# Windowed attention and a gated MLP on one core: the scores of packs 1 to 4 from 128-row products, and another order of the first exponent passes

## Chip, cores and metric

One Trainium2 chip, one core of it. The number is the device time of one execution in microseconds (us); each kernel is run several times and the median stands for it. A profiled execution gives the trace that the rows below come from.

## What is computed

The reference, cut to what matters. The inputs are q, k, v of shape (8, 8, 576, 64) and three weights of 512 x 1536 and 1536 x 512, all float32.

```python
window, dilation, scale = 32, 4, 1.0 / np.sqrt(64)
scores = scale * np.matmul(q, k.transpose(0, 1, 3, 2))
rel = pos[:, None] - pos[None, :]
mask_plain = (rel >= 0) & (rel < window)
mask_dil = (rel >= 0) & (rel < window * dilation) & (rel % dilation == 0)
# heads 0 to 3 use mask_plain, heads 4 to 7 mask_dil
attn = softmax(np.where(masks, scores, -1e9))
x = (attn @ v).transpose(0, 2, 1, 3).reshape(4608, 512)
g = x @ w_gate
out = (g * sigmoid(g) * (x @ w_val)) @ w_out
```

## The kernel before, in words

**Attention comes in packs.** A pack is a tile of queries and keys of four heads: two halves (partitions 0 to 63 and 64 to 127 hold the 64 features of one half each), four blocks of 32 queries in each half, each against its 64 keys. Packs alternate between the plain and the dilated heads. The code counts them from 0 (`m`), and so does this text. For one pack, `scores` adds a mask to the bank `two` by two products with an identity (for the first six packs) and then makes 32 small products of 64 rows, 32 queries and 63 keys. `shift` takes the row maximum away, `exps` exponentiates, `turn_e` transposes on TensorE, `keys` copies the transposed tile out of PSUM, `results` makes 32 products with the values, `norm` divides, `turn_y` transposes on VectorE, and `x_copy` writes the high and the low part of x. A float32 product of this kind is two weight loads and two matmuls in the trace.

**The MLP comes in items.** An item is 512 columns of x (256 in the first six) times 128 columns of the gate and value weights (`gv_mm` into banks `bg`, `bv`) and then times the output weights (`out_mm` into the four banks `bo`). Each product is done in three terms of high and low parts. Weights arrive as bit patterns in units `u` of 128 x 1536 words. Five stages turn a unit into high and low parts: E (exponent, ScalarE), T and B (shift and bits), H (high part, ScalarE), L (low part, GpSimd or VectorE). Item t needs units 2t and 2t+1 for t below 3.

**What sets the order.** Up to the first item's products the order is written by hand: the string `START` is read from left to right, one letter a step (q, v and w issue loads on SyncE's queue, Q scores, S shift, X exps, T turn_e, K keys, A results, N norm, U turn_y, H and L the parts of x, W the next stage of a weight unit, I and J products on a dummy bank). After that, the class `Desk` takes all the instructions in the order of the code and reorders those of every engine but TensorE by its own costs and due times; TensorE keeps the order of the code. In that code `attend(now)` stands between the products of the items: `EARLY`, `LATER` and the lists behind them say at which `now` a pack's visits A (results of the pack before, scores of this one), B (transposes) and C (copies) stand. `Desk.used` remembers for every 32 bytes of a tile's columns who wrote them last, without regard to partitions, and makes a later writer wait for that one.

**Loads.** A load on SyncE's queue waits for the one eight before it on the same queue (eight semaphores in turn), and for whatever still reads its target. The tile of queries and keys of packs 0, 2, 4, 5 is one place, that of packs 1 and 3 another.

Of the kernel before, what the change touches and what calls it, by code (L numbers as in the profile page):

```python
# [12 lines left out]
I32 = mybir.dt.int32  # L13
# [5 lines left out]
P = 128  # L19
# [38 lines left out]

NCS = 3
NSTART = 2  # L60
HALVED = 3
WARM = 9
TURNED = 20
FREE = 16000, 19500, 17500, 18000, 6000
EARLY = (-1, 1, None), (2, 4, 3), (5, 8, 6)
MASKED = 6
X_LOW, W_LOW, H_LOW, KEYS = (3, 7), (1, 5), (5,), (2,)
ON_ACT = (2, 3, 4, 5, 6, 9, 11, 12, 15, 17, 19, 21, 23)
START = ("q0 q1 w v0 v1 w Q0 Q1 S0 X0 T0 W0 I3 I2 S1 K0 X1 W1 A0 W2 T1 J2 K1 W3 J2 N0 W0 w U0 q2 v2 A1 q3 w w r W4 H0 "
         "L0 N1 U1 H1 L1 W1 v3 W2 W3 W4")  # L70
LATER = (14, 3, 2), (23, 3, 4), (29, 7, 4), (39, 3, 2)
T0 = NPLAIN * CH
# [9 lines left out]
class Pack:  # L82
# [5 lines left out]
    def __init__(self, half, strided, part, rest=0):  # L88
        self.half, self.strided, self.part, self.rest = half, strided, part, rest
        self.tail = half == NB  # L90
        self.step = DIL if strided else 1
        self.qstep = BQ
        n = BQ
        if not strided:
            if self.tail:
                self.at = [[(4 * part + 2 * i + g // 2, CH + BQ * (g % 2), 96 * (g // 2) + BQ * (g % 2)) for g in range(NG)]
                           for i in range(2)]
            else:
                self.at = [[(half, 256 * part + P * i + BQ * g, BQ * g) for g in range(NG)] for i in range(2)]
        elif self.tail:  # L100
            n, self.qstep = BQ // 2, BQ // 2
            self.at = [[(4 * rest + g, CH + 2 * part + i, 48 * g) for g in range(NG)] for i in range(2)]
        elif half == 0:
            self.at = [[(0, 2 * i + g // 2 + 256 * part + P * (g % 2), 96 * (g // 2) + BQ * (g % 2)) for g in range(NG)]
                       for i in range(2)]
        else:
            self.at = [[(half, 2 * part + i + DIL * BQ * g, BQ * g) for g in range(NG)] for i in range(2)]
        self.n = n
        self.qwidth = self.qstep * (NG - 1) + BQ
        self.kwidth = max(k for _, _, k in self.at[0]) + BK  # L110
        self.cols = NH * (self.qwidth + self.kwidth)
        first = ["".join("oF"[q < BQ * self.step] for _, q, _ in x) for x in self.at]
        self.mask = MASKS.index(first[0])
        self.mask_step = 0 if first[1] == first[0] else NG
        assert MASKS[self.mask + self.mask_step:][:NG] == first[1]

    def q_at(self, g, j):
        return self.qwidth * j + self.qstep * g

    def k_at(self, i, g, j):  # L120
        return NH * self.qwidth + self.kwidth * j + self.at[i][g][2]
# [13 lines left out]


PACKS = packs()
NPK = len(PACKS)
QKB = max(x.cols for x in PACKS)

# [13 lines left out]
class Desk:  # L154
# [28 lines left out]
    def places(self, ap):  # L183

        t, size = ap.tensor, mybir.dt.size(ap.dtype)
        key = t.name, ap.offset, tuple(map(tuple, ap.ap)), size
        if key not in self.found:
            blocks = ()
            if not isinstance(t, bass.DRamTensorHandle):
                blocks = 0,  # L190
                if ap.space == bass.MemoryType.DRAM:
                    blocks = ap.offset // (P * PIECE),
                elif ap.space != bass.MemoryType.PSUM:
                    at = np.zeros(1, np.int64) + ap.offset % ap.ap[0][0]
                    for step, n in ap.ap[1:]:
                        at = (at[:, None] + step * np.arange(n)).reshape(-1)
                    blocks = tuple(np.unique(at * size // 32).tolist())
                if t.name not in self.users:
                    self.users[t.name] = {}
                    r = getattr(t, "manual_sbuf_range", None) or (0, 0)  # L200
                    self.span[t.name] = r
                    self.under[t.name] = [x for x, (a, e) in self.span.items() if a < r[1] and r[0] < e and x != t.name]
                    for x in self.under[t.name]:
                        self.under[x].append(t.name)
            self.found[key] = t.name, blocks
        return self.found[key]
# [120 lines left out]
def attention_moe(ctx, tc, qkb, vb, w, const, out):  # L327
# [80 lines left out]
    raw_of = {}  # L408
    YW = 3 * UT + 8

    def w_load(parts=2):
        nonlocal loaded
        u = loaded
        n = u % 5 if u < NU - NLAST else (u - NU + NLAST) % NRAW
        if u >= NU or raw_of.get(n, -1) >= done["B" if u < NU - 1 else "L"]:
            return False
        raw_of[n] = u
        loaded += 1
        t = at(raw_at[n], 2 * WU, I32)
        n = 2 * WU // parts  # L420
        for k in range(parts):
# [125 lines left out]
    def masks_of(m, i):  # L547
        n = BK * (pk(m).mask + i * pk(m).mask_step)
        return mask_sb[:, n:n + BK * NG].rearrange("q (g k) -> q g k", g=NG)[:, :, 1:]

    def scores(m, two, masked):

        t = st[m]["qk"]
# [17 lines left out]
    def shift(m, two, pool, masked):  # L571
        mx = pool["bm"](2 * NG).rearrange("q (i g) -> q i g", i=2)
        e = pool["e"]()
        ev = e.rearrange("q (g i k) -> q i g k", g=NG, i=2)[:, :, :, 1:]
        s = two[:, :, SA:].rearrange("q i (g k) -> q i g k", g=NG)
        if not masked:
            n = BK * pk(m).mask
# [225 lines left out]
    nc.vector.memset(ones, 1.0)  # L803
    nc.vector.memset(some, 0.0)
    nc.scalar.activation(out=some, in_=some, func=AF.Exp)
    clear_e(early)
    nc.vector.tensor_copy(out=ident16, in_=eye)
    for n, x in enumerate(MASKS[:4]):
        nc.vector.tensor_copy(out=mask_sb[:, BK * n:BK * n + BK], in_=two_masks[:, BK * "Fo".index(x):][:, :BK])
# [4 lines left out]
    def idle(n, bank=k_bank[1]):  # L814
# [19 lines left out]
        "w": lambda m: w_load(3), "r": lambda m: ready.update(w=True), "I": lambda n: idle(n), "J": lambda n: idle(n, k_bank[0]), "W": lambda n: w_one(STAGES[n]),  # L834
    }

    et = mybir.EngineType
# [39 lines left out]
    def attend(now):  # L877
        for what, m in visit.get(now, ()):
            r = ended(m)
            if what == "A":  # L880
                if r is not None:
                    results(r, two)
                if m < NPK:
                    scores(m, two, m < MASKED)
                if r is not None:
                    norm(r, two, pool_of(r))
# [13 lines left out]
            elif what == "B":  # L900
                if TURNED <= m < NPK:
                    turn_far(m, later)
                elif m < NPK:
                    turn_e(m, two[:, 1])
                    keys(m, two[:, 1], pool_of(m))
            elif r is not None:
                x_copies(r)

# [226 lines left out]
    for t, it in enumerate(items):  # L1135
# [8 lines left out]
        mixing(t, 0)  # L1144
        if not late and t:
            out_mm(before, False)
        gv_mm(it, 1)
        dve_h(it)
        h_hi(it)
# [56 lines left out]
def layout(q, k, v, moe_w_gate, moe_w_val, moe_w_out):  # L1206
# [3 lines left out]
    for m, pk in enumerate(PACKS):  # L1210
        for i, blocks in enumerate(pk.at):
            for g, (b, q0, _) in enumerate(blocks):
                qt = q0 + pk.step * np.arange(pk.n)
                kt = q0 + pk.step * np.arange(-BQ, BQ)
                a, e = int((kt < 0).sum()), int((kt < S).sum())
                for j in range(NH):
                    h, r, qc, kc = NH * pk.strided + j, D * i, pk.q_at(g, j), pk.k_at(i, g, j)
                    qkb[m, r:r + D, qc:qc + pk.n] = q[b, h, qt].T
                    qkb[m, r:r + D, kc + a:kc + e] = k[b, h, kt[a:e]].T
                    vb[m, r + a:r + e, NH * g + j, :D] = v[b, h, kt[a:e]]  # L1220
# [28 lines left out]
```

## Time and profile before

| | |
|---|---|
| median of 3 runs | 911.08 us (909.94 to 911.4) |
| profiled execution | 914.47 us, its span 912.7 us |
| TensorE (PE) busy in the span | 897.8 us, 98% |
| VectorE (DVE), ScalarE (ACT), GpSimd (POOL) busy | 646.0, 382.5, 257.8 us |
| granted TensorE clock, mean | 0.996 of full |

The busy time of TensorE is 98% of the span, so what counts is the time in which it waits or runs at the lower clock; the other engines matter where TensorE waits for them. 1.8 us of the profiled time lie around the span.

### The profile page before, as it was taken

The page shows a single profiled execution, that of the slowest core. Times are in us where ns is not written, and L with a number is a line of the kernel's source. Part 1 is how long each engine was busy: PE and PEld are TensorE (multiplying, and loading weights), DVE is VectorE, ACT ScalarE, POOL GpSimd, SP SyncE. Part 2 cuts the span into 40 slices and gives each one's busy share as a digit, 9 for nine tenths or more (in the row PEclk, how much of TensorE's full clock was granted, in tenths as well). Part 3 has the DMA queues.
Part 4 walks back from the last instruction along what each step waited for, and adds up shares of the span by engine and source line. Part 5 has one row for each costly group of instructions (what it writes and reads, how often), then busy time and mean ns, then how long its engine had stood idle before and what let it go on. Part 6 is the DMA issues. An engine that isn't in the chain of part 4 may idle for free.

```text
span 912.7 us, 20897 instructions
## 1 busy us (share of the span) xinstructions
PE 897.8 (98%) x8642; PEld 737.0 (81%) x8642; DVE 646.0 (71%) x993; ACT 382.5 (42%) x593; POOL 257.8 (28%) x177
## 2 busy tenths in 40 slices
PE   6899999999999999999999999999999999999998
PEld 4798888888888888888888888888878888888886
DVE  5687779888795473777789766878787746555752
ACT  4788433333243242333336544333345533334452
POOL 2468712221311112012032630111146501213451
PEclk9899999999999999999999999999999999999999
DMA  9899986453464640887888678989866675565562
GB/s 338 326 337 368 373 287 224 153 184 122 164 239 146 211 162 13 265 288 263 291 272 282 233 247 279 306 279 296 273 211 222 212 240 198 188 199 189 193 223 92
DMA packets 90382, 214.24 MB, mean 235 GB/s; under 512 B 9264, under 2 KB 32432, under 8 KB 90288
## 3 DMA queue, kind: packets, MB, share of 16 engines
q1 hardware_dynamic: 79776, 208.09, 66.2%
q10 hardware_dynamic: 10512, 4.82, 2.0%
q8 instruction: 68, 1.11, 0.5%
q14 instruction: 26, 0.21, 0.1%
HBM read 165.69 MB, written 47.19 MB: 233 GB/s over the span
## 4 chain that ended last, share of the span: by engine, by line
PE 96%; DMA 2%; issue 1%; SPq 0%; ACT 0%; DVE 0%; POOL 0%; ACTq 0%
PE bo L250 43%; PE bg L250 23%; PE bv L250 23%; PE two L250 7%; DMA at_int<-w 1%; DMA at_float<-turned 1%; SPq L234 0%; DVE at_float L250 0%; POOL at_float32r L234 0%; ACT at_float32r L250 0%; ACT at_float32r L234 0%; ACT at_float L250 0%; ACT at_int L234 0%; ACTq L234 0%
## 5 line engine op out<-in xcount | busy, mean ns | idle before, releaser
L250 PE MATMUL bo<-at_float32r 128*128 128x512 f32 x1296 | 305.7, 390 | 0.0
L250 PEld LDWEIGHTS bo<-at_float32r 128*128 128x128 f32 x1296 | 242.6, 188 | 51.0
L250 POOL TENSOR_TENSOR at_float32r<-at_float,at_float32r 128x512 fp32r<-128x512 f32 (+1 forms) x109 | 161.0, 1480 | 388.7 <-ACT at_float32r L250 210.4
L250 ACT CAST at_float32r<-at_float 128x512 fp32r<-128x512 f32 (+2 forms) x214 | 147.9, 705 | 146.6 <-DVE at_float L250 69.9
L250 DVE TENSOR_TENSOR at_float<-bo,at_float 128x512 f32<-128x512 f32 x168 | 114.1, 683 | 99.7 <-ACT at_float L250 63.7
L250 DVE TENSOR_TENSOR at_float32r<-at_float,at_float32r 128x512 fp32r<-128x512 f32 (+1 forms) x105 | 108.9, 1051 | 48.2 <-ACT at_float32r L250 38.1
L250 PE MATMUL bv<-at_float32r 128*128 128x512 f32 x486 | 128.6, 391 | 0.0
L250 PE MATMUL bg<-at_float32r 128*128 128x512 f32 x486 | 128.3, 390 | 0.0
L250 ACT ACTIVATE at_float<-at_float 128x512 f32<-128x512 f32 (+1 forms) x108 | 67.9, 630 | 134.7 <-DVE at_float L250 121.4
L250 PE MATMUL bg<-at_float32r,at_float32r 128*128 128x512 f32 (+1 forms) x468 | 108.8, 382 | 1.8 <-ACT at_float32r L234 1.2
L250 POOL TENSOR_TENSOR at_float<-at_float,at_float 128x512 f32<-128x512 f32 x36 | 51.3, 1424 | 209.8 <-DVE at_float L250 190.8
L250 PE MATMUL bv<-at_float32r,at_float32r 128*128 128x512 f32 (+1 forms) x468 | 107.2, 379 | 0.0
L250 DVE SCALAR_TENSOR_TENSOR at_float<-at_float,at_float 128x512 f32<-128x512 f32 x144 | 106.1, 743 | 1.1
L250 PE MATMUL bo<-at_float32r,at_float32r 128*128 128x512 f32 (+1 forms) x468 | 106.8, 377 | 0.0
L250 PEld LDWEIGHTS bg<-at_float32r 128*128 128x128 f32 x486 | 90.9, 188 | 19.1
L250 PEld LDWEIGHTS bv<-at_float32r 128*128 128x128 f32 x486 | 90.8, 188 | 19.2
L250 PEld LDWEIGHTS bg<-at_float32r,at_float32r 128*128 128x128 f32 x468 | 83.7, 192 | 18.5 <-ACT at_float32r L234 1.4
L250 PEld LDWEIGHTS bv<-at_float32r,at_float32r 128*128 128x128 f32 x468 | 83.3, 191 | 15.8
L250 PEld LDWEIGHTS bo<-at_float32r,at_float32r 128*128 128x128 f32 x468 | 82.8, 188 | 16.4 <-POOL at_float32r L250 0.2
L250 ACT COPY at_float<-bg 128x512 f32<-128x512 f32 x63 | 37.0, 587 | 84.8 <-PE bg L250 79.9
L250 DVE TENSOR_TENSOR at_float<-at_float,at_float 128x512 f32<-128x512 f32 (+2 forms) x80 | 63.8, 806 | 2.4 <-POOL at_float L250 1.2
L250 ACT COPY at_float<-bv 128x512 f32<-128x512 f32 x63 | 37.1, 589 | 36.9 <-PE bv L250 36.1
(73 smaller groups left out, 610.0 us busy)
## 6 DMA issues: line engine op xcount, KB each, us to landing
at_float32r<-pieces SPq DMA_DIRECT2D x189, 512.0 KB, 4.2
pieces<-at_float32r SPq DMA_DIRECT2D x126, 256.0 KB, 4.2
at_float<-qkb SPq DMA_DIRECT2D x32, 576.0 KB, 6.2
at_float<-vb SPq DMA_DIRECT2D x34, 520.0 KB, 5.4
at_int<-w SPq DMA_DIRECT2D x38, 384.0 KB, 6.2
out<-at_float SPq DMA_DIRECT2D x36, 256.0 KB, 4.3
turned<-at_float SPq DMA_DIRECT2D x18, 256.0 KB, 4.8
at_float<-turned ACTq DMA_DIRECT2D x72, 64.0 KB, 5.2
```

The costliest lines, as they stand in the source:

```text
L250: self.kept.append([engine, lambda: f(*a, **k), sorted(m for m in after if m >= 0), cost, later, both, start])
```

## The change

Packs 1 to 4 get a tile of their own each (packs 1 and 3 one place, 2 and 4 another; `wide_at`, in the room of weight units 16 to 19). The first half's features go to the even partitions and the second half's to the odd ones, by two loads of 64 partitions each. The queries of both halves share columns. The keys of the two halves have columns of their own, and on the other half's partitions these columns hold zeros, which are written once at the start. So one product of 128 rows, 32 queries and 2 x 63 keys gives the scores of both halves: 16 products a pack instead of 32. The halves' columns overlap in the tile: the first load writes columns 0 to 1151 and the second 640 to 1791 (packs 2, 4).

```diff
+WIDE = 1, 5
-EARLY = (-1, 1, None), (2, 4, 3), (5, 8, 6)
+EARLY = (-1, 1, None), (2, 3.5, 3), (5, 8, 6)
+BEFORE = 3
-START = "q0 q1 w v0 v1 w Q0 Q1 S0 X0 T0 W0 I3 I2 S1 K0 X1 W1 A0 W2 T1 J2 K1 W3 J2 N0 W0 w U0 q2 v2 A1 q3 w w r W4 H0 "
+START = "q0 y q1 w v0 v1 w Q0 Q1 S0 X0 T0 W0 I4 S1 K0 X1 W1 A0 W2 T1 J2 K1 W3 J2 N0 w U0 q2 v2 A1 q3 w w r W4 H0 W0 "
...
+    def clear_wide(n):
+        t, x = wide_at[n % 2], pk(n)
+        k = x.cols - NH * x.qwidth
+        (nc.vector if n == 1 else nc.gpsimd).memset(t[:, :k], 0.0)
+        nc.gpsimd.memset(t[:, x.cols:x.cols + k], 0.0)
...
     def load_qk(m, pool, engine, parts=1):
+        if pk(m).wide:
+            t, x = wide_at[m % 2], pk(m)
+            for i in range(2):
+                r, a = slice(D * i, D * i + D), (x.cols - NH * x.qwidth) * i
+                engine.dma_start(out=t[i::2, a:a + x.cols], in_=qkb[m, r, :x.cols])
+            st[m]["qk"] = t
+            return
...
+    def scores_wide(m, two):
...
+        for b in range(2):
+            for j in range(NH):
+                for a in range(2):
+                    g = 2 * a + b
+                    q, k = far + x.q_at(g, j), x.k_at(0, g, j) - NH * x.qwidth
+                    nc.tensor.matmul(out=two[BQ * j:BQ * j + BQ, a, SA + 2 * BU * b:SA + 2 * BU * (b + 1)],
+                                     lhsT=t[:, q:q + BQ], rhs=keys[:, :, k + 1:k + BK], start=False,
+                                     stop=b == 1, skip_group_check=True)
...
             if what == "A":
+                if m == BEFORE:
+                    scores(m, two, m < MASKED)
                 if r is not None:
                     results(r, two)
-                if m < NPK:
+                if m < NPK and m != BEFORE:
                     scores(m, two, m < MASKED)
...
-                    turn_e(m, two[:, 1])
-                    keys(m, two[:, 1], pool_of(m))
+                    turned_at = bank_o[3] if m == BEFORE - 1 else two[:, 1]
+                    turn_e(m, turned_at)
+                    keys(m, turned_at, pool_of(m))
...
+        attend(3 * t + 0.5)
         gv_mm(it, 1)
```

The letter y issues the first third of weight unit 0 ahead of pack 1's data. In `START`, the exponent pass (E) of unit 1, a `W0`, moves behind `H0`. Pack 3's scores come before pack 2's results, pack 2's transposes go to a bank `bo` that is still free, and pack 3's transposes come before the value products of item 1 instead of after them.

First place: SyncE's queue, from the load of weight unit 6 on (tile `at_1536_int_155` before, `at_1536_int_160` now). Before:

```order
L234 DMA at_1536_int_155<-w 128x768 [waits DMAHW2_49,DVE_49,Activation_49]
L234 DMA at_1536_int_155<-w 128x768 [waits DMAHW3_49]
L250 DMA pieces<-at_1536_float32r 128x2x256 [waits DMAHW4_49,Pool_49]
L250 DMA at_1280_float_139<-qkb 128x1152 [waits DMAHW5_49,PE_49]
L250 DMA at_1040_float_149<-vb 128x1040 [waits DMAHW6_49,PE_49]
L250 DMA at_1536_int_294<-w 128x768 [waits DMAHW7_49,DVE_49]
L250 DMA at_1536_int_294<-w 128x768 [waits DMAHW0_49]
L250 DMA at_1536_int_337<-w 128x768 [waits DMAHW1_49,DVE_49]
L250 DMA at_1536_int_337<-w 128x768 [waits DMAHW2_49]
L250 DMA at_1280_float_139<-qkb 128x1152 [waits DMAHW5_49,DMAHW3_49,PE_49]
```

Here the first `qkb` row is pack 4 and the second pack 5, into the same place. Now (`at_2560_float_96` is pack 4, `at_1280_float_145` pack 5):

```order
L244 DMA at_1536_int_160<-w 128x768 [waits DMAHW2_49,DVE_49,Activation_49]
L244 DMA at_1536_int_160<-w 128x768 [waits DMAHW3_49]
L260 DMA at_1280_float_145<-qkb 128x1152 [waits DMAHW4_49]
L260 DMA at_2560_float_96<-qkb 64x1152 [waits DMAHW5_49,PE_49]
L260 DMA at_1040_float_154<-vb 128x1040 [waits DMAHW6_49,PE_49]
L260 DMA at_1536_int_281<-w 128x768 [waits DMAHW7_49,DVE_49]
L260 DMA at_1536_int_281<-w 128x768 [waits DMAHW0_49]
L260 DMA at_1536_int_324<-w 128x768 [waits DMAHW1_49,DVE_49]
L260 DMA at_2560_float_96<-qkb 64x1152 [waits DMAHW2_49]
L260 DMA at_1536_int_324<-w 128x768 [waits DMAHW3_49]
```

Pack 5 no longer waits for TensorE to be done with pack 4 and stands ahead of it. The two halves of pack 4 stand apart, with values, unit 7 and half of unit 8 between them.

Second place: TensorE between the value products of item 0 and the gate products of item 1. Before, and then now (the load and the product with `at_384_bfloat_60`, the mask, stand twice each time and are shown once):

```order
L250 MATMUL bv<-at_1024_float32r,at_1536_float32r 128x256 x12
L250 MATMUL two<-at_192_bfloat_61,at_512_float_124 128x128 x4
L250 MATMUL two<-at_1040_float_149,at_512_float_241 32x65 x32
L250 LDWEIGHTS at_384_bfloat_60
L250 MATMUL two<-at_384_bfloat_60 128x252
L250 MATMUL two<-at_1280_float_142 32x63 x32
L250 MATMUL bg<-at_1024_float32r,at_1536_float32r 128x256 x12
```

```order
L260 MATMUL bv<-at_1024_float32r,at_1536_float32r 128x256 x12
L260 MATMUL bo_382<-at_192_bfloat_61,at_512_float_128 128x128 x4
L260 LDWEIGHTS at_384_bfloat_60
L260 MATMUL two<-at_384_bfloat_60 128x252
L260 MATMUL two<-at_2560_float_97 32x126 x16
L260 MATMUL two<-at_1040_float_154,at_512_float_229 32x65 x32
L260 MATMUL bg<-at_1024_float32r,at_1536_float32r 128x256 x12
```

The results (32x65) moved behind the scores of pack 3, and the scores are 16 products of 126 columns instead of 32 of 63.

## Rows read from the trace of the kernel before

**Rows 1.** The page's first part: busy us, share of the span, instructions.
```profile
PE 897.8 (98%) x8642; PEld 737.0 (81%) x8642; DVE 646.0 (71%) x993; ACT 382.5 (42%) x593; POOL 257.8 (28%) x177
```

**Rows 2.** Stretches: busy us of each engine, granted clock, transfer share, GB/s.
```profile
100.00:500.00 400.00, 400.00 (x4378) 326.94 (x4377) 296.55 (x482) 144.64 (x218) 81.09 (x56) 1.00 0.62 216
500.00:900.00 400.00, 399.32 (x2846) 329.28 (x2845) 272.95 (x397) 168.84 (x276) 119.43 (x81) 1.00 0.70 231
```

**Rows 3.** TensorE's waits in the whole span: us in total, times, longest.
```profile
PE two L250 <- issue: 3.8, 2, 2.0
...
PE two L250 <- DVE at_float L250: 0.8, 1, 0.8
...
PE two L250 <- ACT at_float L250: 0.7, 1, 0.7
```

**Rows 4.** Timeline, TensorE's weight loads alone, between the two pauses.
```profile
21.30 0.14 PEld L250 LDWEIGHTS two<-at_float 64*32 64x32 f32 x4 [2.04 <-issue]
21.54 0.77 PEld L250 LDWEIGHTS bg<-at_float32r,at_float32r 128*128 128x128 f32 x6
22.24 2.20 PEld L250 LDWEIGHTS bv<-at_float32r,at_float32r 128*128 128x128 f32 x12
...
24.38 0.80 PEld L250 LDWEIGHTS two<-at_bfloat,at_float 128*128 128x128 f32 x4
...
26.37 0.70 PEld L250 LDWEIGHTS two<-at_float,at_float 64*32 64x32 f32 x64 [1.19 <-DVE at_float L250]
...
27.16 0.11 PEld L250 LDWEIGHTS <-at_bfloat 128*128 128x128 bf16 x2
...
27.48 0.43 PEld L250 LDWEIGHTS two<-at_float 64*32 64x32 f32 x35 [0.21 <-DMA at_int<-w]
```

**Rows 5.** The page's DMA queues: packets, MB, share of 16 engines.
```profile
q8 instruction: 68, 1.11, 0.5%
```

**Rows 6.** Stretches around the two pauses; columns as in rows 2.
```profile
19.00:22.00 3.00, 1.11 (x44) 0.87 (x34) 1.78 (x3) 2.43 (x3) 1.52 (x1) 1.00 1.03 386
22.00:26.00 4.00, 3.58 (x21) 3.18 (x19) 2.59 (x5) 3.05 (x5) 1.14 (x1) 0.60 1.04 390
...
29.70:33.00 3.30, 3.00 (x40) 2.83 (x41) 2.14 (x5) 0.81 (x2) 0.79 (x1) 0.50 1.03 419
...
36.00:40.00 4.00, 3.33 (x143) 2.69 (x142) 2.01 (x4) 3.28 (x6) 2.94 (x3) 1.00 0.20 74
```

**Rows 7.** Timeline of SyncE's queue: start, time, transfers issued.
```profile
26.52 0.33 SPq L250 DMA_DIRECT2D at_float<-qkb  x1
...
28.46 3.05 SPq L250 DMA_DIRECT2D at_int<-w  x4
39.36 0.33 SPq L250 DMA_DIRECT2D at_float<-qkb  x1
```

**Rows 8.** Transfers issued in 24.4–25.5 and 31–32 us: KB each, us to landing.
```profile
at_int<-w SPq DMA_DIRECT2D x2, 384.0 KB, 6.8
...
at_int<-w SPq DMA_DIRECT2D x1, 384.0 KB, 8.1
```

**Rows 9.** Timeline of TensorE: a wide dummy product, pack 4's scores, item 2.
```profile
13.09 1.08 PE L234 MATMUL fk<-at_float 128*64 128x256 f32 x4
...
38.48 0.85 PE L250 MATMUL two<-at_float 64*32 64x63 f32 x64
39.26 0.98 PE L250 MATMUL bg<-at_float32r,at_float32r 128*128 128x256 f32 x6
```

**Rows 10.** Timeline, GpSimd and ScalarE ahead of the first item; then a clearing.
```profile
14.59 1.74 POOL L234 TENSOR_TENSOR at_float32r<-at_int,at_float32r 128x768 fp32r<-128x768 f32 x1 [13.71 <-ACT at_float32r L234]
...
15.12 0.90 ACT L234 ACTIVATE at_int<-at_int 128x768 f32<-128x768 f32 x1 [0.61 <-DMA at_int<-w]
15.91 0.61 ACT L234 CAST at_float32r<-at_float 128x512 fp32r<-128x512 f32 x1
...
L250 POOL MEMSET at_float<- 128x1024 f32 x2 | 1.8, 954 | 3.0 <-PE bv L250 3.0
```

More of the change, by code (lines that the diff above doesn't have):

```diff
@@ L68 @@
 ON_ACT = (2, 3, 4, 5, 6, 9, 11, 12, 15, 17, 19, 21, 23)
-START = ("q0 q1 w v0 v1 w Q0 Q1 S0 X0 T0 W0 I3 I2 S1 K0 X1 W1 A0 W2 T1 J2 K1 W3 J2 N0 W0 w U0 q2 v2 A1 q3 w w r W4 H0 "
+START = ("q0 y q1 w v0 v1 w Q0 Q1 S0 X0 T0 W0 I4 S1 K0 X1 W1 A0 W2 T1 J2 K1 W3 J2 N0 w U0 q2 v2 A1 q3 w w r W4 H0 W0 "
          "L0 N1 U1 H1 L1 W1 v3 W2 W3 W4")
@@ L111, in __init__ @@
         self.cols = NH * (self.qwidth + self.kwidth)
+        self.wide = False
         first = ["".join("oF"[q < BQ * self.step] for _, q, _ in x) for x in self.at]
@@ L118, in q_at, with widen @@
         return self.qwidth * j + self.qstep * g
+    def widen(self):
+        self.wide = True
+        assert all(a[2] == b[2] for a, b in zip(*self.at))
     def k_at(self, i, g, j):
@@ L137 @@
 PACKS = packs()
+for x in PACKS[slice(*WIDE)]:
+    x.widen()
 NPK = len(PACKS)
@@ L193, in places @@
                 elif ap.space != bass.MemoryType.PSUM:
-                    at = np.zeros(1, np.int64) + ap.offset % ap.ap[0][0]
+                    at = np.zeros(1, np.int64) + ap.offset % (int(np.prod(t.shape[1:])) * mybir.dt.size(t.dtype) // size)
                     for step, n in ap.ap[1:]:
@@ L409, in attention_moe, with w_piece @@
     YW = 3 * UT + 8
+    def w_piece(u, k, parts):
+        n = 2 * WU // parts
+        t = at(raw_at[u], 2 * WU, I32)
+        nc.sync.dma_start(out=t[:, n * k:n * k + n], in_=w[u // 2, u % 2].bitcast(I32)[:, n * k:n * k + n])
     def w_load(parts=2):
@@ L420, in w_load @@
         n = 2 * WU // parts
-        for k in range(parts):
+        for k in range(u == 0, parts):
             nc.sync.dma_start(out=t[:, n * k:n * k + n], in_=w[u // 2, u % 2].bitcast(I32)[:, n * k:n * k + n])
@@ L529, in attention_moe @@
         early[k] = later[k] = Ring(2 * NG, a, a + 2 * NG)
-    def load_qk(m, pool, engine, parts=1):
+    wide_at = [at(M_W + 2 * WU * n, 2 * max(x.cols for x in PACKS[slice(*WIDE)])) for n in (16, 18)]
+    def clear_wide(n):
+        t, x = wide_at[n % 2], pk(n)
+        k = x.cols - NH * x.qwidth
+        assert pk(n + 2).cols == x.cols and x.cols + k <= t.shape[1]
+        (nc.vector if n == 1 else nc.gpsimd).memset(t[:, :k], 0.0)
+        nc.gpsimd.memset(t[:, x.cols:x.cols + k], 0.0)
+    def load_qk(m, pool, engine, parts=1):
+        if pk(m).wide:
[5 more added lines that the diff above has]
+            return
         t = pool["qk"]()
@@ L549, in masks_of @@
         return mask_sb[:, n:n + BK * NG].rearrange("q (g k) -> q g k", g=NG)[:, :, 1:]
+    def scores_wide(m, two):
+        t, x = st[m]["qk"], pk(m)
+        n = BK * x.mask
+        for a in range(2):
+            if x.mask_step:
+                mk = mask_sb[:, n:n + 2 * BK * NG].rearrange("q (i g k) -> q g i k", i=2, g=NG)[:, 2 * a:2 * a + 2, :, 1:]
+            else:
+                mk = masks_of(m, 0)[:, 2 * a:2 * a + 2].unsqueeze(2).broadcast_to([P, 2, 2, BU])
+            nc.tensor.matmul(out=two[:, a, SA:].rearrange("q (b i k) -> q b i k", b=2, i=2), lhsT=ident16, rhs=mk,
+                             start=True, stop=False, skip_group_check=True)
+        far = x.cols - NH * x.qwidth
+        keys = t[:, :2 * x.cols].rearrange("p (i c) -> p i c", i=2)
+        for b in range(2):
+            for j in range(NH):
+                for a in range(2):
+                    g = 2 * a + b
[3 more added lines that the diff above has]
+                                     stop=b == 1, skip_group_check=True)
     def scores(m, two, masked):
+        if pk(m).wide:
+            assert masked
+            return scores_wide(m, two)
         t = st[m]["qk"]
@@ L574, in shift @@
         ev = e.rearrange("q (g i k) -> q i g k", g=NG, i=2)[:, :, :, 1:]
+        if pk(m).wide:
+            ev = e.rearrange("q (a n k) -> q a n k", a=2, n=NG)[:, :, :, 1:]
         s = two[:, :, SA:].rearrange("q i (g k) -> q i g k", g=NG)
@@ L805, in attention_moe @@
     nc.scalar.activation(out=some, in_=some, func=AF.Exp)
+    clear_wide(1)
     clear_e(early)
+    clear_wide(2)
     nc.vector.tensor_copy(out=ident16, in_=eye)
@@ L833, in attention_moe @@
         "v": lambda m: load_v(m, fa, nc.sync, 2),
-        "w": lambda m: w_load(3), "r": lambda m: ready.update(w=True), "I": lambda n: idle(n), "J": lambda n: idle(n, k_bank[0]), "W": lambda n: w_one(STAGES[n]),
+        "w": lambda m: w_load(3), "y": lambda m: w_piece(0, 0, 3), "r": lambda m: ready.update(w=True), "I": lambda n: idle(n), "J": lambda n: idle(n, k_bank[0]), "W": lambda n: w_one(STAGES[n]),
     }
@@ L1217, in layout @@
                     h, r, qc, kc = NH * pk.strided + j, D * i, pk.q_at(g, j), pk.k_at(i, g, j)
+                    if pk.wide:
+                        qc, kc = qc + (NH * pk.kwidth if i == 0 else 0), kc - (NH * pk.qwidth if i == 0 else 0)
                     qkb[m, r:r + D, qc:qc + pk.n] = q[b, h, qt].T
```

## The prediction

> **What bounds the kernel now.** First the page's busy times [rows 1]: TensorE works in 98% of the span, and no other engine in more than 71%. So TensorE's own work is the bound almost everywhere, and a change of order can only give or take the time in which TensorE waits. Then the stretches [rows 2]: from 100 to 500 us it is busy in 400.0 of 400 us, and from 500 to 900 us in 399.3, at the full clock. Nothing can be won there, and whatever is lost ahead of it stays lost, since TensorE has no pause behind in which to catch up. What can move lies ahead of some 45 us. The waits say what is there [rows 3]: two pauses of 3.8 us together, put down to "issue" (no semaphore), and waits of 0.8 and 0.7 us for the copies of two transposed packs.
>
> The pauses stand inside the scores of packs 2 and 3. I count the weight loads between them [rows 4]: 4 + 6 + 12 + 4 + 64 + 2 + 35 = 127, and each has its matmul: 254 instructions. The instruction queue of the page moves 1.11 MB in 68 packets [rows 5], and TensorE has 2 x 8642 = 17,284 such instructions [rows 1], so 254 to a packet. Both pauses are therefore TensorE at the end of a block of instructions with the next one not there. Each also cost clock: behind each, the granted clock stands at 0.60 in the mean of four us and at 0.50 [rows 6], the lower of the two levels (1.2 instead of 2.4 GHz). Full speed lost there is 0.40 x 4.0 = 1.6 us and 0.50 x 3.3 = 1.65 us.
>
> The Trainium skill (Runtime: NRT & Kernel Launch, Instruction fetch mechanics) says that instructions come in blocks of 256, which the trace agrees with, and that the fetch is hidden because dispatch is slower, which the two pauses [rows 3] contradict.
>
> **The change, part by part.**
>
> *Clearings.* Three of 640 or 768 columns on GpSimd, one on VectorE. A clearing of 1024 columns took 0.95 us [rows 10], so GpSimd's take 0.6 + 0.6 + 0.7 = 1.9 us by width. GpSimd stands idle for 13.71 us ahead of its first real work at 14.59 [rows 10], and VectorE waits for the constants. Only the first two stand ahead of a load, and SyncE comes to that load about 2 us in. Price nothing; without that cover, up to 0.7 us on pack 1.
>
> *y.* 256 KB go ahead of pack 1's data. At 390 GB/s [rows 6] pack 1 lands 0.7 us later. Unit 0's last byte stands where it stood, and the copies of the first packs stand behind its exponent pass on ScalarE. Between nothing and 0.7 us; I take 0.2, since that pass is still the later of the two.
>
> *W0 behind H0.* ScalarE waited 0.61 us for unit 1 and worked 0.8 us on it before it began the high part of x at 15.91 [rows 10]. That part now starts some 0.8 us earlier; the low part follows on GpSimd, which is busy with unit 0 until 14.59 + 1.74 = 16.3 [rows 10], so 0.3 us are left of it.
>
> *Pack 3's scores ahead of pack 2's results, pack 3's transposes ahead of the value products.* They put other work into the waits of 0.8 and 0.7 us [rows 3]: 1.5 us.
>
> *Fewer instructions.* A pack's scores go from 128 instructions to 64, four times. A block of instructions then ends where TensorE has long products or has to wait anyway. If both pauses go, 3.8 us and the clock behind them, 3.2 us.
>
> *The wide product itself.* No row shows 128 rows by 32 columns. Now 64 matmuls of 63 columns take 0.78 us (38.48 to 39.26 [rows 9]). Four float32 matmuls of 256 columns on all rows took 1.08 us [rows 9], or 0.22 each if some 0.2 is taken off for the end of the last; so one of 126 columns takes 0.108, and 32 of them 3.5 us one after the other. They go to four groups of 32 columns in turn. Side by side in fours: 0.87 us. Below: 0.78 us, as now. Above: 3.5 us. Since today's small ones (0.054 each by their columns) run 4.4 at a time (64 x 0.054 / 0.78), I take a value near the low end, 0.95 us.
>
> The skill's rule on this speaks against the change: a weight load overlaps matmuls in flight only where its row group differs (TensorE: Matmul & The Clock Gate, The mechanism), and wide products all use every row. By it nothing overlaps, and the price would be 3.5 us or more. The trace has loads on all rows hidden behind products on all rows: the loads of the 12 gate products between the pauses [rows 4] lie under their matmuls.
>
> *Pack 4's data.* This decides. Take TensorE's path with all the gains above: scores of pack 4 at 38.48 today, less 3.8 of pauses, 3.2 of clock, 1.5 of copies, 0.3 of x, plus some for wide products and for waits that come in place of them: between 30 and 33 us. These scores read both halves of pack 4. The halves overlap in the columns of the tile, `Desk` makes the second wait for the first, and it stands five transfers later on SyncE's queue. Ahead of it is pack 5 too, which no longer waits for pack 4's scores (it did, until 39.36 [rows 7]).
>
> When does the second half land? The queue is full: 386 to 419 GB/s and a share of 1.03 to 1.04 until 33 us [rows 6]. Unit 6 lands 6.8 us after its issue at 24.50 and 25.14, so at 31.3 and 31.9 [rows 8]. Behind unit 6 come pack 5 (576 KB), a half of pack 4 (288), values (520), unit 7 (768), half of unit 8 (384) and the second half (288): 2824 KB, or 2.89 MB. At 410 GB/s that is 7.0 us: landing at 38.9 to 39.1. A second way: the transfer eight ahead of it is unit 6's first half, so it can't be issued before 31.3, and one issued at 31.2 took 8.1 us to land [rows 8]: 39.3. I take 39.1. Below: before the change about as many bytes were through by 36.8 in the mean of the 16 engines (a share of 0.20 in 36 to 40 is 0.8 us of a full one [rows 6]); the landing at 39.3 is that of the slowest. If none lagged: 36.7. Above: 39.7.
>
> So TensorE comes to pack 4's scores around 32, and stands until 39.1. All the gains above are spent in this wait.
>
> *The clock.* A pause of 2 us was enough for 3.3 us at half clock. Six or seven us will do it too: from 39.1 on, half speed. Lost: 1.6 us as after each pause, up to 2.5 if it takes half as long again to come back. I take 1.9.
>
> *Behind it.* TensorE's rows are the same from item 2 on. VectorE's x of pack 3 follows pack 4's scores as before, with one more operation ahead (0.95 us), and is covered by the slower products. SyncE runs on where it stood from 31.5 to 39.36 [rows 7], so weights come earlier, and nothing waits for them.
>
> **The sum.** Item 2's gate products began at 39.26 [rows 9]. Now: 39.1 + 0.95 + 1.9 = 41.95. That is 2.7 us later, and nothing behind gives it back: 914.5 + 2.7 = 917.2 us by the profiled execution. That execution was 3.4 us over the median of the runs, so I put the 2.7 on the median: 911.1 + 2.7 = **913.8 us**. Bounds: 36.7 + 0.78 + 1.6 = 39.1, so -0.2 (910.9); 39.7 + 3.5 + 2.5 = 45.7, so +6.4 (917.5).
>
> **Rivals.**
>
> *The second half is there in time.* If it landed by 33, TensorE would not wait: item 2 at 39.26 - 3.8 - 3.2 - 1.5 - 0.3 + 4 x 0.2 (wide products) = 31.3 at best; waits for units 3 to 5, which VectorE and ScalarE still prepare then, would take some of it, so about 34: -5, or **906 us**. For it: all gains are real rows. Against it: 2.89 MB would have to move in 2 us; the queue is full. It decides at a landing of 36.4 (36.4 + 0.95 + 1.9 = 39.25): only an earlier one leaves a gain. By the skill's rule that fetches are hidden, the pauses would be something else and could stay. Then only 1.5 + 0.3 - 0.8 = 1.0 us would be in it, 910.
>
> *It lands early, since the slowest engine lags less:* 36.7 to 38.2, products in 0.8, 1.6 of clock: -0.2 to +1.3, **911.6 us**. Against it: the lag of the slowest engine shows in the 8.1 us of [rows 8].
>
> *Wide products one after the other:* 39.1 + 3.5 + 1.9 = 44.5, +5.2: **916.3 us**. For it: same rows, same column group four matmuls in a row. Only pack 4's count; those of packs 1 to 3 lie ahead of the wait.
>
> **Chances.** The forecast (+1.8 to +4) 0.50, one after the other 0.10, early landing 0.26, in time 0.14. A measurement of this kernel can tell 0.2%, 1.8 us, from no change. Faster by more: 0.14. Within: 0.26. Slower: 0.60. The range leaves out most of the rival that is in time and the upper end of the slow one: 909.5 to 917.0; the likeliest case alone 912.9 to 915.1.
>
> **What the profile would show.** Right: a wait of 5 us or more of TensorE in `two`, put down to a transfer of `qkb` ending near 39, granted clock 0.5 behind it, item 2's gate products from 40.5 on; no pause called issue ahead of it; wide products of 126 columns, 32 matmuls in about 1 us. Wrong: no such wait, or item 2 begun before 38. The forecast falls if the second half lands before 36.4, or if TensorE has a wait behind 45 us today that these rows do not show.

## The result, and the profile after

| | median of the runs | a profiled execution |
|---|---|---|
| before | 911.2 us (909.9 to 911.4, 4 runs) | 914.47 us, span 912.7 |
| changed | 918.0 us (917.3 to 918.6, 4 runs) | 917.3 us, span 915.5 |

The ratio of the runs is 1.0072 (95% interval 1.0057 to 1.0088): the changed kernel is 6.8 us slower. The forecast of 913.8 (909.5 to 917.0) had the sign and missed the size. By the two profiled executions the difference is only 2.8 us, and the forecast for that one was 2.7. Why these two differ is the main thing to find.

The page's first part of the changed kernel, as in [rows 1]: TensorE has 130 matmuls and 130 weight loads fewer, and works as long.

```profile
PE 898.2 (98%) x8512; PEld 737.0 (81%) x8512; DVE 651.0 (71%) x994; ACT 382.1 (42%) x593; POOL 263.4 (29%) x180
```

TensorE's waits in the whole span (us in total, times, longest), which answer to [rows 3]:

```profile
PE two L260 <- DMA at_float<-qkb: 4.1, 2, 3.7
PE two L244 <- issue: 2.2, 1, 2.2
...
PE bo L260 <- issue: 0.7, 1, 0.7
```

A wait for `qkb` is there that was not. Early in the program there is one "issue" pause and not two, in another place: inside pack 1's results. TensorE's timeline (start, us, [idle before <- releaser]) shows the places and answers to [rows 9]:

```profile
13.47 0.60 PE L244 MATMUL two<-at_float,at_float 64*32 64x65 f32 x37 [0.41 <-ACT at_float32r L244]
16.26 0.45 PE L244 MATMUL two<-at_float,at_float 64*32 64x65 f32 x27 [2.19 <-issue]
...
25.64 1.10 PE L260 MATMUL two<-at_float 128*32 128x126 f32 x32
26.67 0.86 PE L260 MATMUL two<-at_float,at_float 64*32 64x65 f32 x64
...
34.25 0.39 PE L260 MATMUL two<-at_bfloat 128*128 128x252 bf16 x2
38.33 1.46 PE L260 MATMUL two<-at_float 128*32 128x126 f32 x32 [3.69 <-DMA at_float<-qkb]
39.72 2.85 PE L260 MATMUL bg<-at_float32r,at_float32r 128*128 128x256 f32 x12
42.41 1.60 PE L260 MATMUL bo<-at_float32r,at_float32r 128*128 128x256 f32 x12
...
45.64 1.20 PE L260 MATMUL bg<-at_float32r,at_float32r 128*128 128x256 f32 x8
47.33 0.74 PE L260 MATMUL bg<-at_float32r,at_float32r 128*128 128x256 f32 x4 [0.49 <-DVE at_float32r L260]
47.91 0.28 PE L260 MATMUL bv<-at_float32r,at_float32r 128*128 128x256 f32 x1
```

Pack 3's 32 wide products take 1.03 us (25.64 to 26.67). TensorE is done with pack 4's masks at 34.6 and stands until 38.3. SyncE's timeline and the transfers issued at 29.9 to 30.2 (KB each, us to landing) show what for (compare [rows 7, 8]):

```profile
30.04 0.48 SPq L260 DMA_DIRECT2D at_float<-qkb  x1
...
at_float<-qkb SPq DMA_DIRECT2D x1, 288.0 KB, 8.2
```

Issued at 30.04 and 8.2 us long: the second half of pack 4 lands at 38.3. Two stretches, the wait and what follows (columns as in [rows 2], the clock third from the end), answer to [rows 6]:

```profile
34.60:38.30 3.70, 0.04 (x1) 0.00 (x0) 2.65 (x3) 3.56 (x5) 2.78 (x3) 1.00 1.03 402
38.30:42.40 4.10, 4.07 (x44) 3.70 (x45) 4.10 (x7) 1.67 (x2) 1.74 (x1) 0.58 1.03 389
```

Behind the wait the clock is 0.58 in the mean of 4.1 us, so most of it at the lower level (1.2 GHz), and item 2's twelve gate products take 2.85 us where item 1's took 1.70. The queue is full in both stretches (a share of 1.03).

### The profile page after: what moved, and what is told of

Same layout as the page of the kernel before. It is cut to its first block, busy times and chain, and to the rows that moved or that the text cites. A ratio compares the mean times of both kernels' runs of the same rounds, so it can differ in the third digit from the quotient of the medians.

```text
span 915.5 us, 20652 instructions
## 1 busy us (share of the span) xinstructions
PE 898.2 (98%) x8512; PEld 737.0 (81%) x8512; DVE 651.0 (71%) x994; ACT 382.1 (42%) x593; POOL 263.4 (29%) x180
## 4 chain that ended last, share of the span: by engine, by line
PE 93%; DMA 4%; DVE 1%; ACT 1%; issue 1%; POOL 0%; SPq 0%; DVEq 0%; ACTq 0%; POOLq 0%
PE bo L260 41%; PE bg L260 22%; PE bv L260 22%; PE two L260 6%; DMA at_float<-turned 2%; DMA at_float<-qkb 1%; DMA at_int<-w 1%; DVE at_float L260 0%; DMA turned<-at_float 0%; ACT at_float32r L260 0%; POOL at_float32r L244 0%; PE two L244 0%; POOL at_float L244 0%; ACT at_float32r L244 0%; DVE at_float L244 0%
## 5 line engine op out<-in xcount | busy, mean ns | idle before, releaser
L260 POOL TENSOR_TENSOR at_float32r<-at_float,at_float32r 128x512 fp32r<-128x512 f32 (+1 forms) x109 | 163.0, 1498 | 392.4 <-ACT at_float32r L260 211.6
L260 DVE TENSOR_TENSOR at_float32r<-at_float,at_float32r 128x512 fp32r<-128x512 f32 (+1 forms) x105 | 113.8, 1098 | 65.5 <-ACT at_float32r L260 55.7
L260 DVE TENSOR_TENSOR at_float<-at_float,at_float 128x512 f32<-128x512 f32 (+2 forms) x80 | 66.8, 844 | 2.4 <-POOL at_float L260 1.2
```

Of the source, the lines that this page charges most:

```text
L260: self.kept.append([engine, lambda: f(*a, **k), sorted(m for m in after if m >= 0), cost, later, both, start])
```

## The experiments

Theory A: the late second half of pack 4, with what follows from it, makes the loss. Rival C: wide products, or the new order on the other engines, make it. A further question is why the runs of before are shorter than its profile. Ratios are to runs of before on the same chip in the same series.

**The kernel before, profiled again** (no edit).

> The kernel before, unchanged, profiled once more. Theory A (the profiled execution of before had two pauses of TensorE and two half-clock spells behind them, 3.2 us, that its timed runs, 3.3 us shorter, do not have): a profile at 910 to 912 us shows item 2's gate products at about 36 instead of 39.26, and one spell or none. Theory B (the two are alike up to item 2, and the 3.3 us lie elsewhere): item 2 within 0.5 us of 39.26 and the difference behind 45 us. By A the changed kernel is slower by 2.7 + 3.3 = 6 us against the timed runs, as measured.

Ratio 1.0006 (0.9993 to 1.0018), profiled execution 910.52 us. Its TensorE timeline:

```profile
19.43 1.05 PE L250 MATMUL two<-at_float 64*32 64x63 f32 x64
...
26.41 0.85 PE L250 MATMUL two<-at_float 64*32 64x63 f32 x64
...
34.79 1.70 PE L250 MATMUL bg<-at_float32r,at_float32r 128*128 128x256 f32 x12
...
39.57 1.73 PE L250 MATMUL bg<-at_float32r,at_float32r 128*128 128x256 f32 x12
41.14 1.59 PE L250 MATMUL bv<-at_float32r,at_float32r 128*128 128x256 f32 x12
```

The 64 matmuls of pack 2's scores, and of pack 3's, run in one piece: both pauses of [rows 3] are gone in the same program. Item 2 begins at 34.79, 4.5 us ahead of [rows 9], and the execution is 4.0 us shorter. Theory A of this run holds. (This execution has half clock too, from 20 to 24 us (granted clock 0.50 and 0.74), so by item 2 the two differ by 4.5 us and not by all of the pauses and their clock.) Of 73 runs of before in the three series, 6 are at 913 us or more: an execution as long as that of [rows 1 to 10] is rare. That the runs near the median lack its pauses is seen in this one profile. Against this profile the changed kernel's loses 4.9 us up to item 2 (39.72), 1.15 in its gate products (2.85 for 1.70), 0.7 in item 3 (45.64 to 47.91 is 2.27, here 1.57): 6.8 us by item 3's value products (47.91 and 41.14), as much as the medians differ by.

**The halves of pack 4 next to each other.**

```diff
     def take(self, engine, what, a, k):
...
+        if self.twin is not None:
+            after.discard(self.twin)
+            self.twin = None
...
             for i in range(2):
+                if i and nc.kept is not None:
+                    nc.twin = len(nc.kept) - 1
                 engine.dma_start(out=t[i::2, a:a + x.cols], in_=qkb[m, r, :x.cols])
```

> The changed kernel, but the second half of a wide pack does not wait for its first half in the planner, so pack 4's halves stand next to each other on SyncE's queue. Theory A (the late second half and the half clock behind it are what the change loses): the second half lands near 34.3 instead of 38.3, TensorE's wait of 3.7 us in front of pack 4's scores shrinks below 0.5, the clock stays up, item 2 begins at 35.5 to 36.5 instead of 39.7, and the time is 912 to 913.5, 5 us below the changed kernel. Rival C (wide products or the new order on the other engines cost it; the wait only takes up slack): another wait, for weight units or for x, stands in its place, and the time is 916 to 918.

911.5 us, ratio 1.0021 (1.0008 to 1.0034). TensorE's timeline and, last, the two transfers issued at 25.2 to 26.5:

```profile
16.03 0.45 PE L244 MATMUL two<-at_float,at_float 64*32 64x65 f32 x27 [1.64 <-issue]
...
33.99 0.39 PE L263 MATMUL two<-at_bfloat 128*128 128x252 bf16 x2
34.31 1.10 PE L263 MATMUL two<-at_float 128*32 128x126 f32 x32
35.35 1.70 PE L263 MATMUL bg<-at_float32r,at_float32r 128*128 128x256 f32 x12
...
at_float<-qkb SPq DMA_DIRECT2D x2, 288.0 KB, 7.6
```

The wait is gone and the clock stays up: item 2 is 4.4 us earlier and the profiled execution (912.3 us) 5.0 us shorter; the medians stand 1.2 us over before instead of 6.8. The wide products and the new order are as they were, so theory A holds for all but 0.2%.

**The wide packs alone, in the order of before.**

```diff
-EARLY = (-1, 1, None), (2, 3.5, 3), (5, 8, 6)
-BEFORE = 3
+EARLY = (-1, 1, None), (2, 4, 3), (5, 8, 6)
+BEFORE = None
...
-START = "q0 y q1 ... I4 S1 ... W4 H0 W0 "
+START = "q0 q1 ... I3 I2 S1 ... N0 W0 ... W4 H0 "
...
```

> The wide packs alone, with the order of before (pack 3's scores behind pack 2's results, transposes in the old bank, no first third of unit 0 ahead of pack 1, exponent pass of unit 1 where it was). The second half of pack 4 stands as late on SyncE's queue. Theory A: TensorE comes to pack 4's scores some 1.5 us later and waits that much less; 917 to 919, as the whole change. Rival C (the order costs it): 911 to 913.

918.7 us, 1.0094 (1.0081 to 1.0107): as expected by A. TensorE waits 3.3 us for the second half.

**The new order alone, narrow packs** (the same lines of the change, without `WIDE` and y).

> The new order alone, with the narrow packs of before (pack 4 is one load of 128 partitions again; the first third of unit 0 is not moved). Theory A: no late half, the two waits for copies of transposed packs are filled, 909 to 911. Rival C (the order costs it): 914 to 918.

910.3 us, 0.9998 (0.9987 to 1.0010). The order costs nothing and gives nothing either. Its timeline:

```profile
33.69 0.85 PE L251 MATMUL two<-at_float 64*32 64x63 f32 x64 [0.57 <-DMA at_float<-qkb]
34.47 1.70 PE L251 MATMUL bg<-at_float32r,at_float32r 128*128 128x256 f32 x12
...
40.66 0.74 PE L251 MATMUL bg<-at_float32r,at_float32r 128*128 128x256 f32 x4 [0.22 <-DVE at_float32r L251]
```

Item 0 begins 2.5 us earlier than in the second profile of before (14.91 and 17.40), item 2 only 0.3: waits for packs' data (1.8 us in 3) took the place of those for copies.

**The late half alone, in the kernel before.**

```diff
     def load_qk(m, pool, engine, parts=1):
...
+        if m == 4:
+            for i in range(2):
+                engine.dma_start(out=t[D * i:D * i + D, :n], in_=qkb[m, D * i:D * i + D, :n])
+            st[m]["qk"] = t
+            return
```

> The kernel before, with one edit: pack 4 is loaded in two halves of 64 partitions each, same bytes, same narrow products. The planner makes the second half wait for the first, so that it stands five places later on SyncE's queue, with values, unit 7 and half of unit 8 between. Theory A (the late second half alone makes the loss): it lands at 36.8 to 37.8 instead of 33.7, TensorE waits some 3 us for it, the clock falls, and the time is 914.5 to 916.5, 4 to 6 us over before. Rival C (wide products or the order): 910 to 911.5, no change.

921.8 us, 1.0119 (1.0105 to 1.0133): one edit of a load, and the time is 10.8 us longer. TensorE's timeline, the transfer issued at 30.54, and two stretches of this run (columns as in [rows 2]):

```profile
34.53 0.29 PE L250 MATMUL two<-at_float 64*32 64x63 f32 x2 [0.35 <-DMA at_float<-qkb]
41.69 1.16 PE L250 MATMUL two<-at_float 64*32 64x63 f32 x62 [6.86 <-DMA at_float<-qkb]
42.78 2.93 PE L250 MATMUL bg<-at_float32r,at_float32r 128*128 128x256 f32 x12
...
at_float<-qkb SPq DMA_DIRECT2D x1, 288.0 KB, 11.1
...
30.00:32.00 2.00, 2.00 (x19) 2.00 (x18) 2.00 (x4) 2.00 (x4) 0.00 (x0) 1.00 1.02 227
36.00:38.00 2.00, 0.00 (x0) 0.00 (x0) 1.39 (x1) 0.08 (x1) 0.74 (x1) 0.87 1.04 198
```

The sign and the mechanism are those of A. The size was off because this half took 11.1 us to land and not 7, and its place in the queue does not explain that: the queue moved 227 and 198 GB/s in the two stretches, at a full share, where the changed kernel's moved 409 and 404 in the same microseconds. A weight transfer of 384 KB into all 128 partitions, issued just ahead of the half, took 11.1 us as well. What sets the loads of this run apart is that the 64 partitions of each half stand next to each other, while those of the wide packs are every other one. With the 8.2 us of the changed kernel the half would have landed at 38.7 (an estimate), some 3 us earlier. So the run shows what a late half does to the kernel before, and not the price of its place alone.

**Pack 4 narrow, packs 1 to 3 wide** (`WIDE = 1, 4`).

> The changed kernel with packs 1 to 3 wide and pack 4 narrow again, so it is one load of 128 partitions on SyncE's queue and not two halves five transfers apart. Theory A (only the late half of pack 4 and the half clock behind it cost): no wait over 0.6 us ahead of pack 4's scores, item 2 at 35 to 36, 911 to 912.5, as with the halves next to each other. Rival C (wide products or the order cost it): 916 to 918.

913.9 us, 1.0037 (1.0021 to 1.0053): 3.4 us under the changed kernel's 917.3 of the same series, but 1.4 over what A expected. The second fence is TensorE's waits from 550 to 690 us, where the second profile of before has none but 1.0 us for `turned`:

```profile
32.70 1.70 PE L260 MATMUL bg<-at_float32r,at_float32r 128*128 128x256 f32 x12
...
37.08 1.70 PE L260 MATMUL bv<-at_float32r,at_float32r 128*128 128x256 f32 x12 [1.25 <-ACT at_int L260]
```

```profile
PE bo L260 <- DVE at_float L260: 1.7, 1, 1.7
PE bo L260 <- issue: 1.1, 1, 1.1
```

Item 2 begins 2.1 us ahead of before (34.79). A wait for a weight unit takes 1.25 of it, and behind 550 us two waits that the second profile of before lacks take 2.8. So in this profile rival C has a part after all, of another kind: small waits far behind the change. That fewer instructions or another plan of the other engines brought them is likely, but not shown. The changed kernel has 0.7 us of them (the second "issue" row above).

**Pack 1 narrow, packs 2 to 4 wide, halves together** (the second experiment, `WIDE = 2, 5`).

> Packs 2 to 4 wide with halves next to each other, pack 1 narrow as before: 64 instructions more of TensorE ahead of pack 1's results, so the end of a block of instructions leaves these results, where it cost the changed kernel 2.2 us (1.6 with the halves together). Theory A1 (that pause and the half clock behind it are what is left of the loss): item 2 1 to 2 us earlier than 35.35, 909 to 910. Theory A2 (the transfers set the pace by now, pack 4's data land near 34 whatever TensorE does before): item 2 at 35.0 to 35.4, 911 to 911.5, as with four wide packs.

914.7 us (912.7 to 917.6), 1.0049 (1.0031 to 1.0068), profiled execution 912.8 us. The pause in pack 1's results is gone, and a wait of 1.48 us for pack 4's data stands at 34.58 in its place; item 2 at 35.61. That is theory A2 in the profile. The median lies above both forecasts, 3 us over the run with four wide packs; this is not explained, since no longer execution of it was profiled.

**Pack 5's load behind pack 4's** (the second experiment, with pack 5's load made to follow pack 4's second half in the planner).

> Four wide packs, pack 4's halves next to each other, and pack 5's load behind them instead of ahead. If the transfers set the pace of pack 4's scores: the second half lands near 33.0 instead of 33.75, and the time is at or up to 0.8 us below that with the halves next to each other, 910.7 to 911.5. If TensorE's pause in pack 1's results sets it: no change, 911.5.

912.7 us, 1.0021 (1.0007 to 1.0034): the same ratio as with the halves next to each other, so no change. TensorE comes to pack 4's scores at 34.42 and finds the data (the trace does not show when they landed); a pause of 0.72 us, in pack 1's results again, and half clock behind it still hold it up until then.

**TensorE kept at work in the wait.** The mask products of pack 4 are made 8 times each, then 20 times each, the same values again.

```diff
-            nc.tensor.matmul(..., lhsT=ident16, rhs=mk, start=True, stop=False, skip_group_check=True)
+            for _ in range(8 if m == 4 else 1):
+                nc.tensor.matmul(..., lhsT=ident16, rhs=mk, start=True, stop=False, skip_group_check=True)
```

> The changed kernel, with the two mask products of pack 4 made eight times each in place of once (the same values again), so that TensorE works through most of its wait for the second half. The landing is not changed. If the clock that falls in the wait costs what the rows show (wide products 1.46 instead of 1.10, twelve gate products of item 2 2.85 instead of 1.70): 1.5 us less than the changed kernel, 916.0 to 917.0. If those rows are long for another reason: 917.5 to 918.5, no change.

> As with eight mask products, which left 4.6 us of the wait empty and the clock fell all the same; now twenty of each (the same values again), some 4.8 us of work. The landing of the second half stays at 37.8 to 38.3. If the half clock behind the wait is a cost of its own: wide products near 1.1 and item 2's twelve gate products near 1.70 us instead of 1.46 to 1.93 and 2.8 to 2.9, time 915.0 to 916.5, 1.5 to 2.5 us below the changed kernel. If not: 917.3 to 918.0.

8 times: 918.0 us, 1.0084 (1.0067 to 1.0101). 20 times: 919.1 us, 1.0086 (1.0072 to 1.0100). The changed kernel itself had 917.3 us and 1.0080 in the series of the first; the 919.1 us lie above both forecasts. The price of 1.5 us or more was not found with 20 either, though the rows came as expected. TensorE's timeline with 8, then with 20:

```profile
31.45 1.92 PE L260 MATMUL two<-at_bfloat 128*128 128x252 bf16 x16
37.97 1.54 PE L260 MATMUL two<-at_float 128*32 128x126 f32 x32 [4.61 <-DMA at_float<-qkb]
39.44 2.78 PE L260 MATMUL bg<-at_float32r,at_float32r 128*128 128x256 f32 x12
```

```profile
33.21 4.54 PE L260 MATMUL two<-at_bfloat 128*128 128x252 bf16 x40
37.68 1.10 PE L260 MATMUL two<-at_float 128*32 128x126 f32 x32
38.71 1.70 PE L260 MATMUL bg<-at_float32r,at_float32r 128*128 128x256 f32 x12
...
45.85 0.50 PE L260 MATMUL bg<-at_float32r,at_float32r 128*128 128x256 f32 x2 [0.60 <-ACT at_float32r L260]
46.98 0.74 PE L260 MATMUL bg<-at_float32r,at_float32r 128*128 128x256 f32 x4 [0.63 <-DVE at_float32r L260]
```

With 8, the execution had no pause in pack 1's results, TensorE came 2.5 us earlier (31.45, with the changed kernel's 33.99 and 34.25), and item 2 began no more than 0.3 us earlier: in these profiles whatever is won ahead of the landing is lost in the wait. With 20, the wait is filled, the clock stays up (1.00 from 37.7 to 42 us), and TensorE is done with item 2's gate products at 40.25, 2.2 us ahead of the changed kernel (42.41). And yet item 3's last gate products start at 46.98, only 0.35 earlier, because they wait for the low part of pack 3's x. VectorE's timeline, first in the second profile of the changed kernel, then with 20, shows where they stand:

```profile
38.73 0.94 DVE L260 TENSOR_SCALAR at_int<-at_int 128x768 int32<-128x768 int32 x1
39.86 0.68 DVE L260 TENSOR_REDUCE at_float<-two 128x8 f32<-128x504 f32 x1 [0.19 <-PE two L260]
...
46.24 1.10 DVE L260 TENSOR_TENSOR at_float32r<-at_float,at_float32r 128x512 fp32r<-128x512 f32 x1 [1.22 <-ACT at_float32r L260]
```

```profile
39.96 0.95 DVE L260 TENSOR_SCALAR at_int<-at_int 128x768 int32<-128x768 int32 x1 [0.91 <-issue]
40.83 0.67 DVE L260 TENSOR_REDUCE at_float<-two 128x8 f32<-128x504 f32 x1
...
45.83 1.09 DVE L260 TENSOR_TENSOR at_float32r<-at_float,at_float32r 128x512 fp32r<-128x512 f32 x1 [0.35 <-ACT at_float32r L260]
```

In VectorE's order the row maximum of pack 4 (39.86) stands ahead of pack 3's division, transpose and low part (46.24), so late scores of pack 4 can hold up pack 3's x too. But they do so by 0.19 us only: until 39.7 VectorE works at stages of weight units. With 20, the scores were done at 38.7, 1.0 us earlier, and the row maximum came 1.0 us later (40.83), behind a pause of VectorE's own of 0.91 us and such a stage. So in this execution the clock that was given back on TensorE is lost in front of pack 3's x, which VectorE's own work held up. Whether it would be a gain without that pause is open.

**Narrow packs in the new order, packs 2 and 3 in places of their own,** so that pack 4's load waits for no products.

```diff
-        t = pool["qk"]()
+        t = at(M_W + 2 * WU * (14 + m), QKB) if m in (2, 3) else pool["qk"]()
```

> The order of the changed kernel with narrow packs, and packs 2 and 3 in places of their own (the room of units 16 to 19), so that pack 4's load waits for no products. If the transfers set the pace once the order is changed: pack 4 lands near 32 instead of 33.65, TensorE does not wait for it, item 2 begins at 32.7 to 33.5 instead of 34.5, and the time is 908.5 to 909.5, below both kernels. If weight units or x hold TensorE next: 910 to 910.5, as with the order alone.

911.2 us, 0.9996 (0.9983 to 1.0008). Its timeline:

```profile
32.68 0.85 PE L251 MATMUL two<-at_float 64*32 64x63 f32 x64 [0.47 <-DMA at_float<-qkb]
33.46 1.70 PE L251 MATMUL bg<-at_float32r,at_float32r 128*128 128x256 f32 x12
...
40.64 0.74 PE L251 MATMUL bg<-at_float32r,at_float32r 128*128 128x256 f32 x4 [0.62 <-DVE at_float32r L251]
```

Pack 4's scores and item 2 are 1.0 us earlier than with the order alone, as expected, and item 3's last gate products start when they did there (40.64 and 40.66): x of pack 3 is next in line. TensorE still waits 0.47 us for the data, and the time lies above both forecasts, level with before (911.0 us in this series). No version beat the kernel before.

**The changed kernel again** (no edit).

> The changed kernel once more, beside these three. Its wait for pack 4's second half ends at 38 to 38.6 by the transfers, so that it is there in every execution: 917.3 to 918.6, ratio to before 1.007 to 1.009.

917.3 us (916.2 to 921.0), 1.0080 (1.0061 to 1.0098), the profiled one 916.4 us: the wait is 3.46 us and ends at 37.84, just ahead of the 38 expected, item 2 begins at 39.70, and its gate products take 2.93 us.

## Why the prediction was right in sign and wrong in size

**The step that failed** is the last of the sum: "That execution was 3.4 us over the median of the runs, so I put the 2.7 on the median." The 3.4 us were no even surplus. As far as the second profile of before shows, they came from the two pauses and the half clock behind them, and the same text counts both as gains that the new wait swallows. A wait that ends at a landing puts rare and common executions at the same place, so the 2.7 belonged on the profiled execution: 917.2 us, which the prediction has one sentence earlier, and which the profiled execution after (917.3) and the median (918.0) bear out. Against the runs that is 2.7 + 3.4 = 6.1; measured 6.8.

That 917.2 came so near to 917.3 is in part luck. By item 3's value products the two profiled executions differ by 2.3 us (47.91, and 45.57 before), and another 0.5 us came far behind:

```profile
45.57 1.60 PE L250 MATMUL bv<-at_float32r,at_float32r 128*128 128x256 f32 x12
```

**The pauses.** That they are the ends of blocks of instructions stands, and counting from the start of TensorE's timeline bears it out: in [rows 3] they come behind the 349th and the 477th matmul, 128 apart; in the changed kernel, and with the wide packs alone in the old order, behind the 221st, again 128 before. (Between the two pauses stand 127 weight loads and 128 matmuls, one more than the prediction counts.) That they are a property of the kernel does not stand: none in a second execution. And the sign "no pause called issue ahead of it" is wrong: the end of a block now lies 37 matmuls into pack 1's results, always at the same place, with 2.19 us of pause in both profiles of the changed kernel, 1.64, 1.85 and 0.72 in others that share this part, and next to none in two. In the changed kernel it costs nothing, since the wait behind it takes it up (the run with 8 mask products).

**The late half** is right, in place, cause and time: landing 38.3 for 39.1 forecast. The wait was 3.7 us and not seven (the prediction's sign was 5 or more), because TensorE came at 34.6 and not near 32 (the pause, and half clock behind it; in the run with 8 mask products, without the pause, it came at 31.45). Item 2 began at 39.72, ahead of the 40.5 given as a sign.

**The wide product:** 1.03 us at the full clock, 0.95 forecast; one after the other (3.5) is out. The Trainium skill's rule that a weight load overlaps only matmuls of another row group (TensorE: Matmul & The Clock Gate, The mechanism) would, as the prediction reads it, make it 3.5 us or more; the trace does not agree.

**The clock:** 1.15 us in item 2's gate products and 0.36 in the wide ones (1.39 for 1.03) make 1.5, just under the bounds of 1.6 to 2.5; in the second profile of the changed kernel 0.83 (1.86 for 1.03), 1.19 (2.73 for 1.54) and 0.62 (output products, 2.06 for 1.44), from start to start, make 2.6, just over them. But the two executions begin item 3's value products at 47.91 and 47.98, so it is no term to be added as it stands: pack 3's low part is ready near 47.3 in both, and what the clock costs ahead of that is covered in part. In the run with 20 mask products the clock given back brought 0.35 us there.

**Behind it.** "Is covered by the slower products" was wrong by 0.5 us: TensorE waits for pack 3's low part in item 3 (47.33). In the second profile of the changed kernel, where the clock cost 1.1 us more, it was right: no such wait stands there. So 39.72 + 1.15 + 0.7 = 41.6 stands for the 41.95 of the sum: the landing 0.8 and the clock 0.4 too long, the rest behind it 0.7 too short.

**The gains of the order** (1.5 us for the two waits for copies) are not there even without the late half: with the order alone 0.9998, since waits for the data of packs 2 to 4, and then for x of pack 3, took their place.

What the halves next to each other still lose, 0.2%, is a pause of 1.6 us with half clock behind it and a wait of 0.65 us for x in its profile; that these make it was not shown by taking them away alone.

## What to carry to other kernels

Before a difference is put on a median, ask which stalls of the profiled execution the others have: a second profile of the unchanged kernel would have shown it. A new wait that ends at a landing is to be reckoned as a moment, not as an amount, and everything won ahead of it is gone. When a load is split, look where each part comes to stand in its queue: here bookkeeping by columns alone made one half wait for the other, and that cost some 5 us, while the wide products won nothing even without it (1.0021).

## What had not been expected of the hardware

- The same program had two pauses of TensorE, 3.8 us together, in one execution and none in another. The Trainium skill (Runtime: NRT & Kernel Launch, Instruction fetch mechanics) says that the fetch is hidden; if the pauses are the fetch, as the counts of matmuls say, it was in one of the two.
- 288 KB into 64 partitions next to each other took 11.1 us to land; into every other partition 8.2 us, issued half a microsecond apart. The whole queue was slower with the first: 198 to 227 GB/s where the other moved 404 to 409, both at a full share, and transfers to 128 partitions beside it landed as late. Only one run has such loads.
- TensorE's clock fell behind a wait of 3.7 us (0.58 in the mean of 4.1 us) and of 4.6, and not where 40 mask products filled the wait (1.00).
